# A fused attention and feed-forward kernel: RMS weight row behind the first q, last block's scores in two banks, sink scores inside score phases, one score phase merged

## The chip, the cores and the metric

The kernel runs on one core of a Trainium2 chip. The metric is the device time of that core in microseconds (us). The core has TensorE (PE in the profile, with its weight loads as PEld), VectorE (DVE), ScalarE (ACT), GpSimd (POOL) and SyncE (SP), which here only issues DMAs. POOL issues DMAs too: those that turn float32 into bfloat16 on the way.

## The reference

There are 4 sequences (b) of 768 positions, 8 heads (h) of width 64, a window of 128 and 4 sink positions.

```python
scores = scale * np.matmul(q, k.transpose(0, 1, 3, 2))
keep = (pos[None, :] < 4) | ((rel >= 0) & (rel < 128))     # rel = query - key
scores = np.where(keep, scores, -1e9)
a = softmax(scores)
attn = np.matmul(a, v)                        # 4, 8, 768, 64
x = attn as 3072 rows of 512
xn = x / sqrt(mean(x * x) + 1e-6) * rms_g
g = xn @ w_gate;  val = xn @ w_val            # 512 -> 1536
out = (g * sigmoid(g) * val) @ w_out          # 1536 -> 512, float32
```

So each query sees the four first keys of its sequence and the 128 latest keys.

## The kernel before, in words

The 3072 rows are cut into 24 blocks (`g`) of 128 positions, six to a sequence (`b, t = divmod(g, 6)`). Four blocks make a group (`G`) of 512 rows for the feed-forward part (FFN); there are six groups.

**Attention of a block.** q and k of the block are loaded and transposed, for blocks 0 to 7 on PE (`pe_t`, L412, with a copy `copy_t`, L421), from block 8 on by DMA transposes that SP issues (`dma_t`, L428). `scores` (L445) multiplies the block's keys with the queries of this block and of the next, since the window reaches back into the block before; it uses four PSUM banks, two heads to a bank. Matmuls of two heads run in pairs on the two halves of PE's rows (64 partitions each). The last block of a sequence (t = 5) has no next block, and fills half of each of its four banks. `exps` (L463) is ACT's exponential, one for each bank; `mask_dve` or, from block 16 on, `mask_pool` cuts the window. `av` (L501) multiplies with v, where a column of ones gives the sum for the softmax. From t = 2 on the sinks lie outside the window, and `av` begins with a matmul for them. Their scores come from `sink_s` (L619), a separate phase of four PE matmuls, each on 32 columns of PE; it makes the sink scores of two blocks at once in sequences 0 and 1, of four blocks (t = 2 to 5) in sequences 2 and 3, and needs those blocks' transposed q. `sink_e` is its exponential.

**Norm.** `normal` (L526), `square` (L537) and `rms` (L545) divide by the softmax's sum and form the RMS norm. The weight row `rms_g` is loaded into one partition (`grow`, L341), spread over 128 partitions by one matmul with ones (`unit_gb`, L398) and scaled by ACT to `gb` (`scale_gb`), which `rms` reads. The block's x is then transposed, on PE for blocks 0 to 8 (`pe_x`, L575), by a DMA transpose on SP from block 9 on (`dma_x`, L590).

**FFN of a group.** A unit (`ffn`, L832) is 16 times 128, 8 times 256 or 4 times 512 columns of g and as many of v, each in a bank; then tanh on ACT (L764) and two DVE operations (L770, L780) give hT. Group 0 is worked in four chunks of 128 rows, groups 1 and 2 in two of 256, the rest whole: 12 units in each group. `project` (L786) multiplies hT with wo, ACT takes the result out of PSUM and SP stores it.

**Who sets the order.** All operations are first given to a planner (`Plan`, L27): each with a cost in ns, what it needs and gives, the banks that it takes and drops, and a priority. The planner walks through time: of all operations whose needs are met it takes the one that can start earliest, with the lower priority number first where two are equal. It models DMA rings too. The resulting list is emitted, so that every engine then runs its instructions in that fixed order. There are eight PSUM banks; an operation that takes k banks can start when k are free. Fill matmuls (`warm`, 30 of them) have the last priority of all.

Needs of note:

- `gate_of(g)` (L640): a block from `GATE_FROM` on scores only after FFN unit `(g // 4 - 1) * 18 + 4 * (g % 4) - GATE_LEAD` (18 units to a group: 12 of FFN and 6 for the projection).
- A DMA transpose of block g's q or k is issued only after the scores of block `g - T_LEAD`, a load of block g (from 10 on) only after the scores of block `g - LOAD_LEAD`.
- The list `LOADS` (L177) is the order of POOL's loads; eight may be under way (`DEPTH`). `w-9-12` loads columns 9 to 12 (in units of 128) of w_gate and then of w_val.
- SP's first three DMAs are in the order of their priorities: k of block 0 (-90), `grow` (-89.5), q of block 0 (-89).

Of the kernel before, what the change touches and what calls it, by code (L numbers as in the profile page):

```python
# [26 lines left out]
class Plan:  # L27
# [3 lines left out]


    LATE = 300
    HOP = {"PE": 40, "ACT": 35, "DVE": 35, "POOL": 90, "SP": 60}
    START = {"PE": 800, "ACT": 800, "DVE": 1030, "POOL": 1290, "SP": 800}

# [32 lines left out]
    def run(self):  # L69
        free, users = dict(self.START), {}  # L70
        self.loads = sum(o["ring"] == "POOL" for o in self.ops)
        wait = {o["at"]: set(o["needs"]) for o in self.ops}
        cand = {e: [] for e in free}
        left = len(self.ops)
        for o in self.ops:
            for t in o["needs"]:
                users.setdefault(t, []).append(o)
            if not o["needs"]:
                for e in o["ways"]:
                    cand[e].append(o)  # L80
        busy, warm, mode, order = [], False, 0, []
        while left:
            first = None
            for e, found in cand.items():
                for o in found:
                    k = len(o["takes"])
                    if k > len(self.banks):
                        continue
                    ready = o["ready"] + self.HOP[e] if o["ready"] else 0
                    if k:  # L90
                        ready = max(ready, sorted(self.banks.values())[k - 1] + 40)
                    start = max(free[e], ready)
                    key = (start, o["prio"], ready, o["at"])
                    if first is None or key < first[0]:
                        first = key, e, o
            if first is None:
                raise RuntimeError("stuck: %s" % [
                    (o["gives"], list(wait[o["at"]])) for o in self.ops if o["at"] in wait
                ][:20])
            (start, *_), e, o = first  # L100
            for x in o["ways"]:
                cand[x].remove(o)
            wait.pop(o["at"])
            left -= 1
            ns, lat, fn = o["ways"][e]
            if e == "PE":
                busy = [(a, d) for a, d in busy if a > start - 3413]
                warm = start - free[e] < 4000 and (warm or sum(d for a, d in busy) > 3000)
                ns = ns if warm else 2 * ns
                if o["mode"] != mode:  # L110
                    ns, mode = ns + 110, o["mode"]
                busy.append((start, ns if mode != 2 else 0))
                lat = ns + 180
            for s in o["takes"]:
                i = min(self.banks, key=lambda i: (self.banks[i], i))
                del self.banks[i]
                self.held[s] = i
            free[e] = start + ns
            end = start + lat
            if o["ring"] is not None:  # L120
                end = self.land(o["ring"], end, o["work"]) + self.LATE
            for s in o["drops"]:
                self.banks[self.held[s]] = end + 12
            for t in o["gives"]:
                for x in users.pop(t, ()):
                    x["ready"] = max(x["ready"], end + 12)
                    w = wait[x["at"]]
                    w.discard(t)
# [8 lines left out]
def kernel(  # L137
# [195 lines left out]
    for i, name in enumerate(F32_LOADS):  # L333
# [5 lines left out]
                "ACT": (640, lambda n=n, g=g: cast(n, g, nc.scalar.copy))},  # L339
               [(n + "st", g), "table"], [(n, g)], -99)  # L340
    op({GROW: (430, 1000, lambda: {"SP": nc.sync, "ACT": nc.scalar}[GROW].dma_start(  # L341
        out=grow, in_=moe_rms_g.rearrange("(o d) -> o d", o=1)))}, (), ["grow"], -89.5,
        ring="HW", work=50)
    act(1290, None, (), ["table"], -80)

# [99 lines left out]
    def scores(g, n0, n1):  # L445
        b, t = divmod(g, NT)
        qkT = T["qkT", b]
        for u in range(2):
            for j in range(2):
                hp = 2 * u + j  # L450
                for hi in range(2):
# [8 lines left out]
                        start=g >= PE_MASKS, stop=True, skip_group_check=True,  # L460
                    )

    def exps(g, u, hi, n0, n1, last):  # L463
        if ("e", g, u) not in T:
            T["e", g, u] = epool.tile([P, 4, 2, P], BF16, name=f"e{u}", bufs=3)
# [35 lines left out]
    def av(g, u):  # L501
# [7 lines left out]
        for j in range(2):  # L509
            for hi in range(2):  # L510
# [3 lines left out]
                if t >= 1:  # L514
                    nc.tensor.matmul(  # L515
                        out=dest, lhsT=T["e", g - 1, u][:, x, 1, :],
                        rhs=V16[b][:, t - 1, h, :],
                        start=(t == 1), stop=False, skip_group_check=True,
                    )
                nc.tensor.matmul(  # L520
                    out=dest, lhsT=T["e", g, u][:, x, 0, :], rhs=V16[b][:, t, h, :],
                    start=(t == 0), stop=True, skip_group_check=True,
                )
        T.pop(("e", g - 1, u), None)
# [104 lines left out]
    def sink_e(b, t, n):  # L629
# [17 lines left out]
    for g in range(NB):  # L647
        b, t = divmod(g, NT)
# [17 lines left out]
                   [(n, g)] + old + [("s", g - T_LEAD)], [(n + "T", g)], g,  # L666
                   ring="TR", work=1000)

        slots = [("s", g, u, hi) for u in range(2) for hi in range(2)]
        parts = [(0, 1), (1, 2)] if g in SPLIT else [(0, nq)]  # L670
        if g < PE_MASKS:
            pe(864, lambda g=g: mask_bias(g), [("bias", 0), ("bias", 1), "ident", "idnos"]
               + ([("qp", g), ("kp", g)] if g else []), [("mb", g)], pa, takes=slots)
        for n0, n1 in parts:
            needs = [("kT", g)] + [("qT", g + i) for i in range(n0, n1)] + gate_of(g)
            needs += [("mb", g)] if g < PE_MASKS else []
            last = (n0, n1) == parts[-1]
            pe(220 * (n1 - n0), lambda g=g, n=(n0, n1): scores(g, *n), needs,
               [("s", g, n0)] + ([("s", g)] if last else []), pa + 1 + n0,
               takes=slots if g >= PE_MASKS and n0 == 0 else (), mode=1)  # L680
            for u in range(2):
                for hi in range(2):
                    act(215 * (n1 - n0) + 55,
                        lambda g=g, u=u, hi=hi, n=(n0, n1), last=last: exps(g, u, hi, *n, last),
                        [("s", g, n0), "table"] + ([("av", g - 2, u)] if g >= 2 else [])
                        + ([("x", g, u, 0, n0)] if hi else []),
                        [("x", g, u, hi, n) for n in range(n0, n1)], early,
                        drops=[("s", g, u, hi)] if last else ())
        for u in range(2):
            xs = [[("x", g, u, hi, n) for hi in range(2)] for n in range(nq)]  # L690
            if g < PE_MASKS:
                es = xs
# [10 lines left out]
            T["es", g, u] = es  # L703
            needs = es[0] + (T["es", g - 1, u][1] if t else []) + [("v", g), ("vone", b)]
            needs += [("v", g - 1)] if t else []
            needs += [("esk", b, t), ("vsk", b, 0), ("vsk", b, 1)] if t >= 2 else []
# [25 lines left out]
        if t == 0:  # L732
# [3 lines left out]
            for half in range(2):  # L736
# [6 lines left out]
            for t0, n in ((2, 2), (4, 2)) if b < 2 else ((2, 4),):  # L743
# [175 lines left out]
```

The softmax here doesn't subtract the row's maximum and nothing guards it: scores larger than these inputs give would overflow.

## Time and profile before

| what | value |
|---|---|
| median of 11 runs | 247.49 us (246.79 to 248.01) |
| the profiled execution's own time | 248.05 us |
| span of that execution, first to last instruction | 246.3 us |
| PE busy | 235.4 us (96%) |
| DVE busy | 183.7 us (75%) |
| ACT busy | 131.0 us (53%) |
| POOL busy | 88.6 us (36%) |
| FFN's matmuls: g, v (L757) and o (L790), busy | 69.5, 71.0 and 62.7 us |
| HBM read and written | 28.31 and 6.29 MB |

A row of the busiest groups reads: line, engine, operation, output and inputs with their shapes, count, then busy us and the mean ns of one, then the engine's idle time before them. Matmuls are pipelined, and a matmul's mean is longer than the distance to the next: an o matmul of 512 columns has a mean of 380 ns, while its successor starts 216 ns after it. What PE's work costs is therefore read from start to start. Records of some matmuls are missing (263 of 276 o matmuls are there). The mean granted clock is 1.00 over the span; the first 18 us still show matmuls at half rate, 107 ns for 128 columns in place of 56.

### The profile page before, as it was taken

The page shows a single profiled execution, that of the slowest core. Times are in us where ns is not written, and L with a number is a line of the kernel's source. Part 1 is how long each engine was busy: PE and PEld are TensorE (multiplying, and loading weights), DVE is VectorE, ACT ScalarE, POOL GpSimd, SP SyncE. Part 2 cuts the span into 40 slices and gives each one's busy share as a digit, 9 for nine tenths or more (in the row PEclk, how much of TensorE's full clock was granted, in tenths as well). Part 3 has the DMA queues.
Part 4 walks back from the last instruction along what each step waited for, and adds up shares of the span by engine and source line. Part 5 has one row for each costly group of instructions (what it writes and reads, how often), then busy time and mean ns, then how long its engine had stood idle before and what let it go on. Part 6 is the DMA issues. An engine that isn't in the chain of part 4 may idle for free.

```text
span 246.3 us, 5510 instructions
## 1 busy us (share of the span) xinstructions
PE 235.4 (96%) x2098; PEld 149.4 (61%) x2120; DVE 183.7 (75%) x482; ACT 131.0 (53%) x276; POOL 88.6 (36%) x114
## 2 busy tenths in 40 slices
PE   4798999999999999999999999999999999999994
PEld 2467998785788775588875444444545444444443
DVE  4178979997899998899889589992299993377700
ACT  3559456778677556555627445834736621333211
POOL 8986755696444559522003300221604100000000
PEclk9999999999999999999999999999999999999999
DMA  7999999999999999999923644013320013200022
GB/s 103 172 168 196 192 187 189 154 140 169 160 199 133 142 128 157 167 203 156 154 23 85 145 107 94 3 21 87 109 64 20 6 21 106 85 3 0 0 85 85
DMA packets 111979, 27.22 MB, mean 110 GB/s; under 512 B 102097, under 2 KB 109009, under 8 KB 111954
## 3 DMA queue, kind: packets, MB, share of 16 engines
q0 software_dynamic: 80704, 13.90, 77.3%
q1 hardware_dynamic: 31106, 12.85, 27.8%
q8 instruction: 16, 0.26, 0.5%
q10 hardware_dynamic: 144, 0.13, 0.2%
q14 instruction: 9, 0.07, 0.1%
HBM read 28.31 MB, written 6.29 MB: 140 GB/s over the span
## 4 chain that ended last, share of the span: by engine, by line
PE 80%; DVE 10%; DMA 4%; issue 3%; ACT 2%; SPq 0%; DVEq 0%; ACTq 0%
PE v L757 21%; PE g L757 21%; PE o L790 21%; PE s L456 4%; DVE hT L780 2%; PE av L520 2%; DMA stage<-in_q_dram 2%; DVE p L770 2%; DVE r L560 2%; DMA xnt<-xr 2%; PE av L515 2%; DVE xr L564 2%; PE av L505 1%; PE o_last L808 1%; DVE x L532 1%
## 5 line engine op out<-in xcount | busy, mean ns | idle before, releaser
L757 PE MATMUL v<-xnt,wv 128*128 128x128 bf16 (+2 forms) x522 | 71.0, 281 | 0.3
L757 PE MATMUL g<-xnt,wg 128*128 128x128 bf16 (+2 forms) x525 | 69.5, 282 | 0.5 <-DMA xnt<-xr 0.4
L764 ACT ACTIVATE th<-g 128x512 bf16<-128x512 f32 x72 | 42.9, 600 | 45.8 <-PE g L757 42.0
L790 PE MATMUL o<-wo,hT 128*128 128x512 bf16 x263 | 62.7, 380 | 1.2 <-issue 0.6
L770 DVE SCALAR_TENSOR_TENSOR p<-th,g 128x512 bf16<-128x512 bf16 x72 | 48.0, 682 | 15.2 <-ACT th L764 14.8
L757 PEld LDWEIGHTS <-wg 128*128 128x128 bf16 x528 | 43.0, 98 | 19.6 <-issue 0.6
L757 PEld LDWEIGHTS <-wv 128*128 128x128 bf16 x528 | 42.6, 98 | 18.5 <-issue 0.8
L469 ACT ACTIVATE e<-s 128x512 bf16<-128x512 f32 (+1 forms) x104 | 48.2, 541 | 8.2 <-PE s L456 8.0
L780 DVE TENSOR_TENSOR hT<-p,v 128x512 bf16<-128x512 bf16 x72 | 47.2, 681 | 1.5 <-PE v L757 0.6
L790 PEld LDWEIGHTS <-hT 128*128 128x128 bf16 x276 | 25.5, 98 | 28.7 <-issue 1.3
L491 POOL TENSOR_SCALAR_AFFINE_SELECT e<-e 128x512 bf16<-128x512 bf16 x14 | 9.4, 678 | 65.2 <-ACT e L469 52.2
L798 ACT ACTIVATE osb<-o 128x512 f32<-128x512 f32 x23 | 13.8, 598 | 29.1 <-PE o L790 29.1
L327 POOL DMA_DIRECT2D v<-in_v_dram x24 | 21.3, 888 | 14.5 <-DMA q<-in_q_dram 8.2
L323 POOL DMA_DIRECT2D q<-in_q_dram x23 | 20.5, 893 | 12.4 <-DMA k<-in_k_dram 3.9
L323 POOL DMA_DIRECT2D k<-in_k_dram x23 | 20.4, 886 | 11.3 <-DMA wo<-in_moe_w_out_dram 3.3
L532 DVE TENSOR_TENSOR x<-av,rden 128x256 bf16<-128x256 f32 x48 | 20.4, 424 | 1.6
L531 DVE RECIPROCAL rden<-av 128x4 f32<-128x4 f32 x48 | 8.5, 176 | 17.1 <-PE av L520 17.1
L540 ACT ACTIVATE sq<-x 128x512 bf16<-128x512 bf16 x24 | 15.1, 631 | 9.7 <-DVE x L532 9.6
L486 DVE TENSOR_TENSOR e<-e,masks 128x1024 bf16<-128x1024 bf16 (+1 forms) x30 | 18.9, 650 | 0.9 <-ACT e L469 0.8
L564 DVE SCALAR_TENSOR_TENSOR xr<-x,r,gb 128x512 bf16<-128x512 bf16 x24 | 19.0, 790 | 0.9
L520 PE MATMUL av<-v,e 128*128 128x65 bf16 x192 | 17.3, 197 | 0.0
L456 PE MATMUL s<-qkT 64*128 64x256 bf16 (+1 forms) x208 | 14.8, 266 | 0.6 <-ACT qkT L423 0.6
(70 smaller groups left out, 183.1 us busy)
## 6 DMA issues: line engine op xcount, KB each, us to landing
out_dram<-osb SPq DMA_DIRECT2D x23, 256.0 KB, 2.2
v<-in_v_dram POOLq DMA_DIRECT2D x24, 128.0 KB, 10.3
q<-in_q_dram POOLq DMA_DIRECT2D x23, 128.0 KB, 10.4
k<-in_k_dram POOLq DMA_DIRECT2D x23, 128.0 KB, 10.4
wo<-in_moe_w_out_dram POOLq DMA_DIRECT2D x2, 768.0 KB, 12.4
wg<-in_moe_w_gate_dram POOLq DMA_DIRECT2D x4, 256.0 KB, 7.2
wv<-in_moe_w_val_dram POOLq DMA_DIRECT2D x4, 256.0 KB, 7.9
wg<-in_moe_w_gate_dram POOLq DMA_DIRECT2D x1, 384.0 KB, 10.2
```

The lines of the kernel that those rows point to most:

```text
L323: nc.gpsimd.dma_start(out=T[name, g], in_=block_of(src, g))
L327: nc.gpsimd.dma_start(out=V16[b][:, t, :, 0:D], in_=block_of(v, g))
L456: nc.tensor.matmul(out=BANK[slot][:, j * 256 + n0 * P:j * 256 + n1 * P], lhsT=qkT[pr, 1, hp, t * P:(t + 1) * P], rhs=qkT[pr, 0, hp, (t + n ...
L469: nc.scalar.activation(out=T["e", g, u][:, 2 * hi:2 * hi + 2, n0:n1, :].rearrange("p x n c -> p x (n c)"), in_=ps.rearrange("p (j c) -> p ...
L520: nc.tensor.matmul(out=dest, lhsT=T["e", g, u][:, x, 0, :], rhs=V16[b][:, t, h, :], start=(t == 0), stop=True, skip_group_check=True,)
L532: nc.vector.tensor_tensor(out=T["x16", g][:, 4 * u:4 * u + 4, :], in0=pvv[:, :, 0:D], in1=rden.unsqueeze(2).to_broadcast((P, 4, D)), op=AL ...
L564: nc.vector.scalar_tensor_tensor(out=T["xr", g], in0=T.pop(("x16", g)).rearrange("p h d -> p (h d)"), scalar=r[:, 3:4], in1=gb, op0=ALU.mu ...
L757: nc.tensor.matmul(out=ps[:, i * n:(i + 1) * n], lhsT=w_sb[:, kt, ft * P:(ft + 1) * P], rhs=T["xnt", G][:, kt, cols], start=(kt == 0), sto ...
L764: nc.scalar.activation(out=T["th", key], in_=BANK[("g", key)], func=ACT.Tanh, scale=0.5,)
L770: nc.vector.scalar_tensor_tensor(out=T["p1", key], in0=T.pop(("th", key)), scalar=1.0, in1=BANK.pop(("g", key)), op0=ALU.add, op1=ALU.mult,)
L780: nc.vector.tensor_tensor(out=T[hk][:, i:i + n, cols], in0=T.pop(("p1", key)).rearrange("p (n c) -> p n c", n=n), in1=BANK.pop(("v", key)) ...
L790: nc.tensor.matmul(out=BANK[("o", G, tb)], lhsT=T["h", G, ft // 4][:, ft % 4, tb * P:(tb + 1) * P], rhs=wo[:, ft, :], start=(ft == 0), sto ...
```

## The change

Eight things are changed.

1. `grow` gets priority -80, so SP issues it behind q of block 0.
2. `w-9-12` becomes `w-9-10 w-10-12`: four loads in place of two.
3. `X_DMA_FROM` goes from 9 to 8: block 8's x is transposed by DMA and not on PE.
4. The last block of a sequence gets functions of its own: eight matmuls into two banks, four heads to a bank; two exponentials of 512 columns in place of four of 256; two masks over 512 columns. `av` reads the new tile.
5. From sequence 2 on (`FUSE_FROM`) the sink scores are no operation of their own: they are emitted at the end of the score phase of block t = 2, whose needs and banks grow by theirs (the transposed q of t = 2 to 5, one bank).
6. `MERGE = (2,)`: the last block of sequence 2 (block 17) has no score phase of its own; its matmuls are put ahead of those of block 18, and the needs and banks of both are joined.
7. `GATE_FROM` 6 to 8, `GATE_LEAD` 6 to 14, `LOAD_LEAD` 9 to 10, `T_LEAD` 3 to 4.
8. The planner gets `RESERVE = 8`: when an operation that takes more than 8 banks is waiting, one with a later priority may not take banks that it would need.

The loop over the blocks keeps its needs otherwise; the part that makes the scores moves into a function `block_scores`.

```diff
+    RESERVE = 8
...
+            many = min(
+                (o for o in cand["PE"] if len(o["takes"]) > self.RESERVE), default=None,
+                key=lambda o: o["prio"],
+            )
...
+                    if (k and many and o["prio"] > many["prio"] and start > many["ready"]
+                            and len(self.banks) - k < len(many["takes"])):
+                        continue
...
-    LOADS = "q-1 k-1 v-0 w-0-2 v-1 qkv-2 qkv-3 w-2-4 w-4-6 w-6-8 w-8-9 w-9-12 qkv-4 wo-0-6 qkv-5 wo-6-12 qkv-6 qkv-8 qkv-7"
+    LOADS = "q-1 k-1 v-0 w-0-2 v-1 qkv-2 qkv-3 w-2-4 w-4-6 w-6-8 w-8-9 w-9-10 w-10-12 qkv-4 wo-0-6 qkv-5 wo-6-12 qkv-6 qkv-8 qkv-7"
-    X_DMA_FROM = 9
+    X_DMA_FROM = 8
-    GATE_FROM = 6
-    LOAD_LEAD = 9
+    GATE_FROM = 8
+    LOAD_LEAD = 10
-    GATE_LEAD = 6
-    T_LEAD = 3
+    GATE_LEAD = 14
+    T_LEAD = 4
+    FUSE_FROM = 2
+    GROW_PRIO = -80
+    MERGE = (2,)
...
-        out=grow, in_=moe_rms_g.rearrange("(o d) -> o d", o=1)))}, (), ["grow"], -89.5,
+        out=grow, in_=moe_rms_g.rearrange("(o d) -> o d", o=1)))}, (), ["grow"], GROW_PRIO,
...
+    def scores_last(g):
...
+        for hp in range(HP):
+            for hi in range(2):
+                pr = slice(hi * D, (hi + 1) * D)
+                nc.tensor.matmul(
+                    out=BANK["s", g, hi][:, hp * P:(hp + 1) * P], lhsT=qkT[pr, 1, hp, cols],
+                    rhs=qkT[pr, 0, hp, cols], start=True, stop=True, skip_group_check=True,
+                )
+    def exps_last(g, hi):
...
+        nc.scalar.activation(
+            out=T["el", g][:, hi * HP:(hi + 1) * HP, :].rearrange("p x c -> p (x c)"),
+            in_=BANK.pop(("s", g, hi)), func=ACT.Exp, scale=inv_sqrt_d,
+        )
...
+    def sink_parts(b):
+        return ((2, 2), (4, 2)) if b < 2 else ((2, 4),)
+    def sink_needs(b, t, n):
+        return [("ksk", b)] + [("qT", b * NT + t + i) for i in range(n)]
...
+            if merged and n0 == 0:
+                more, banks, given, other = merged
+                needs, gives, takes = needs + more, gives + given, takes + banks
+                work.insert(0, lambda g=other: scores_last(g))
...
+            if last and b >= FUSE_FROM:
+                for t0, n in sink_parts(b):
+                    if t0 == t:
+                        needs = needs + sink_needs(b, t0, n)
+                        gives.append(("ss", b, t0))
+                        takes = takes + [("ss", b, t0)]
+                        work.append(lambda b=b, t0=t0, n=n: sink_s(b, t0, n))
...
+            if b in MERGE:
+                merged = (needs, slots, [("s", g, 0), ("s", g)], g)
+            else:
+                pe(220, lambda g=g: scores_last(g), needs, [("s", g, 0), ("s", g)], pa + 1,
+                   takes=slots, mode=1)
...
-                pe(n * 53 + 16, lambda b=b, t0=t0, n=n: sink_s(b, t0, n),
-                   [("ksk", b), ("s", g + 1)] + [("qT", g + t0 + i) for i in range(n)],
-                   [("ss", b, t0)], -1000.0 + 10 * (g + t0) + 2, takes=[("ss", b, t0)], mode=3)
+                if b < FUSE_FROM:
+                    pe(n * 53 + 16, lambda b=b, t0=t0, n=n: sink_s(b, t0, n),
+                       [("s", g + 1)] + sink_needs(b, t0, n), [("ss", b, t0)],
+                       -1000.0 + 10 * (g + t0) + 2, takes=[("ss", b, t0)], mode=3)
```

More of the change, by code (lines that the diff above doesn't have):

```diff
@@ L461, in scores, with mask_dve_last, mask_pool_last @@
                     )
+    def scores_last(g):
+        b, t = divmod(g, NT)
+        qkT = T["qkT", b]
+        cols = slice(t * P, (t + 1) * P)
+        for hi in range(2):
+            bank(("s", g, hi))
+        for hp in range(HP):
+            for hi in range(2):
+                pr = slice(hi * D, (hi + 1) * D)
[4 more added lines that the diff above has]
+    def exps_last(g, hi):
+        if ("el", g) not in T:
+            T["el", g] = epool.tile([P, H, P], BF16, name="e0", bufs=3)
+        nc.scalar.activation(
+            out=T["el", g][:, hi * HP:(hi + 1) * HP, :].rearrange("p x c -> p (x c)"),
+            in_=BANK.pop(("s", g, hi)), func=ACT.Exp, scale=inv_sqrt_d,
+        )
+    def mask_dve_last(g, hi):
+        ev = T["el", g][:, hi * HP:(hi + 1) * HP, :]
+        nc.vector.tensor_tensor(
+            out=ev, in0=ev, in1=masks[:, 1, 0:1, :].to_broadcast((P, HP, P)), op=ALU.mult,
+        )
+    def mask_pool_last(g, hi):
+        ev = T["el", g][:, hi * HP:(hi + 1) * HP, :]
+        nc.gpsimd.affine_select(
+            out=ev, in_=ev, compare_op=ALU.is_ge,
+            fill=0.0, base=0, pattern=[[0, HP], [1, P]], channel_multiplier=-1,
+        )
     def exps(g, u, hi, n0, n1, last):
@@ L519, in av @@
                     )
+                own = (T["e", g, u][:, x, 0, :] if t + 1 < NT
+                       else T["el", g][:, hi * HP + 2 * u + j, :])
                 nc.tensor.matmul(
-                    out=dest, lhsT=T["e", g, u][:, x, 0, :], rhs=V16[b][:, t, h, :],
+                    out=dest, lhsT=own, rhs=V16[b][:, t, h, :],
                     start=(t == 0), stop=True, skip_group_check=True,
@@ L645, in gate_of, with block_scores @@
         return [("F", G, i)] if i < FTN else [("O", G, (i - FTN) * 2 // 3)]
-    for g in range(NB):
+    merged = None
+    def block_scores(g):
+        nonlocal merged
         b, t = divmod(g, NT)
@@ L651 @@
         early = -20.0 + g if g < 2 * GB else 0.1 * g
-        old = []
-        if b >= 2:
-            old = [("s", NT * (b - 2) + i) for i in range(NT)]
-            old += [("ss", b - 2, i) for i in ((2, 4) if b - 2 < 2 else (2,))]
-        for n in "qk":
-            if g < QK_DMA_FROM:
-                pe(225, lambda n=n, g=g: pe_t(n, g), [(n, g), "ident"] + old, [(n + "p", g)],
-                   pa, takes=[(n, g)])
-                ways = {"DVE": (345, lambda n=n, g=g: copy_t(n, g, nc.vector.tensor_copy)),
-                        "ACT": (470, lambda n=n, g=g: copy_t(n, g, nc.scalar.copy))}
-                either(ways, [(n + "p", g), "table"], [(n + "T", g)], early, drops=[(n, g)])
-            else:
-                sp(1290, 1200, lambda n=n, g=g: dma_t(n, g),
-                   [(n, g)] + old + [("s", g - T_LEAD)], [(n + "T", g)], g,
-                   ring="TR", work=1000)
         slots = [("s", g, u, hi) for u in range(2) for hi in range(2)]
@@ L677 @@
             last = (n0, n1) == parts[-1]
-            pe(220 * (n1 - n0), lambda g=g, n=(n0, n1): scores(g, *n), needs,
-               [("s", g, n0)] + ([("s", g)] if last else []), pa + 1 + n0,
-               takes=slots if g >= PE_MASKS and n0 == 0 else (), mode=1)
+            gives = [("s", g, n0)] + ([("s", g)] if last else [])
+            takes = slots if g >= PE_MASKS and n0 == 0 else []
+            ns, work = 220 * (n1 - n0), [lambda g=g, n=(n0, n1): scores(g, *n)]
+            if merged and n0 == 0:
+                more, banks, given, other = merged
+                needs, gives, takes = needs + more, gives + given, takes + banks
+                work.insert(0, lambda g=other: scores_last(g))
+                ns += 220
+                merged = None
+            if last and b >= FUSE_FROM:
[5 more added lines that the diff above has]
+                        work.append(lambda b=b, t0=t0, n=n: sink_s(b, t0, n))
+                        ns += 53 * n + 100
+            pe(ns, lambda work=work: [w() for w in work], needs, gives, pa + 1 + n0, takes=takes,
+               mode=1)
             for u in range(2):
@@ L703 @@
             T["es", g, u] = es
+    for g in range(NB):
+        b, t = divmod(g, NT)
+        nq = 2 if t + 1 < NT else 1
+        pa = -1000.0 + 10 * g
+        early = -20.0 + g if g < 2 * GB else 0.1 * g
+        old = []
+        if b >= 2:
+            old = [("s", NT * (b - 2) + i) for i in range(NT)]
+            old += [("ss", b - 2, i) for i in ((2, 4) if b - 2 < 2 else (2,))]
+        for n in "qk":
+            if g < QK_DMA_FROM:
+                pe(225, lambda n=n, g=g: pe_t(n, g), [(n, g), "ident"] + old, [(n + "p", g)],
+                   pa, takes=[(n, g)])
+                ways = {"DVE": (345, lambda n=n, g=g: copy_t(n, g, nc.vector.tensor_copy)),
+                        "ACT": (470, lambda n=n, g=g: copy_t(n, g, nc.scalar.copy))}
+                either(ways, [(n + "p", g), "table"], [(n + "T", g)], early, drops=[(n, g)])
+            else:
+                sp(1290, 1200, lambda n=n, g=g: dma_t(n, g),
+                   [(n, g)] + old + [("s", g - T_LEAD)], [(n + "T", g)], g,
+                   ring="TR", work=1000)
+        if t + 1 == NT:
+            slots = [("s", g, hi) for hi in range(2)]
+            needs = [("kT", g), ("qT", g)] + gate_of(g)
+            if b in MERGE:
+                merged = (needs, slots, [("s", g, 0), ("s", g)], g)
+            else:
+                pe(220, lambda g=g: scores_last(g), needs, [("s", g, 0), ("s", g)], pa + 1,
+                   takes=slots, mode=1)
+            xs = []
+            for hi in range(2):
+                act(480, lambda g=g, hi=hi: exps_last(g, hi),
+                    [("s", g, 0), "table"] + [("av", g - 2, u) for u in range(2)]
+                    + ([("x", g, 0)] if hi else []), [("x", g, hi)], early, drops=[("s", g, hi)])
+                if g < POOL_MASK_FROM:
+                    dve(335, lambda g=g, hi=hi: mask_dve_last(g, hi), [("x", g, hi), "masks"],
+                        [("e", g, hi)], early)
+                else:
+                    pool(590, lambda g=g, hi=hi: mask_pool_last(g, hi), [("x", g, hi)],
+                         [("e", g, hi)], g)
+                xs.append(("e", g, hi))
+            T["es", g, 0] = T["es", g, 1] = [xs]
+        else:
+            block_scores(g)
+        for u in range(2):
+            es = T["es", g, u]
             needs = es[0] + (T["es", g - 1, u][1] if t else []) + [("v", g), ("vone", b)]
@@ L742 @@
                     [("vsk", b, half)], 0.1 * g, drops=[("vs", b, half)])
-            for t0, n in ((2, 2), (4, 2)) if b < 2 else ((2, 4),):
-                pe(n * 53 + 16, lambda b=b, t0=t0, n=n: sink_s(b, t0, n),
-                   [("ksk", b), ("s", g + 1)] + [("qT", g + t0 + i) for i in range(n)],
-                   [("ss", b, t0)], -1000.0 + 10 * (g + t0) + 2, takes=[("ss", b, t0)], mode=3)
+            for t0, n in sink_parts(b):
+                if b < FUSE_FROM:
+                    pe(n * 53 + 16, lambda b=b, t0=t0, n=n: sink_s(b, t0, n),
+                       [("s", g + 1)] + sink_needs(b, t0, n), [("ss", b, t0)],
+                       -1000.0 + 10 * (g + t0) + 2, takes=[("ss", b, t0)], mode=3)
                 act(n * 107 + 55, lambda b=b, t0=t0, n=n: sink_e(b, t0, n),
```

## The prediction

> **What bounds the kernel now.** I began with the page's first two parts: who is busy, and when.
>
> ```profile
> span 246.3 us, 5510 instructions
> PE 235.4 (96%) x2098; PEld 149.4 (61%) x2120; DVE 183.7 (75%) x482; ACT 131.0 (53%) x276; POOL 88.6 (36%) x114
> ...
> PE   4798999999999999999999999999999999999994
> ...
> DVE  4178979997899998899889589992299993377700
> ```
>
> PE is full in all but the first four slices (25 us) and the last. So I asked next what PE waits for once it is running, in the waits of PE alone from 22.5 us on:
>
> ```profile
> PE o L790 <- issue: 0.6, 4, 0.2
> PE x L579 <- DVE xr L564: 0.4, 1, 0.4
> PE g L757 <- DMA xnt<-xr: 0.4, 1, 0.4
> ```
>
> That is all: 1.4 us in 220. Three of the four "issue" waits are first records missing from a project group (a group of 11 or 7 in place of 12 or 8). Measured from start to start, two real stalls remain: at 141.00 (the last attention matmul starts at 140.44 and could have been followed 0.03 later: 0.53 us) and at 205.35 (two o matmuls 0.51 apart, not 0.216: 0.29 us). Together 0.82 us. The kernel therefore ends when PE has started plus the sum of PE's work. A change can gain in three ways only: start sooner, give PE less work, remove those stalls. It loses by any new wait on PE.
>
> The start I read in the chain of waits of the first 26 us:
>
> ```profile
> 0.81 0.46 SPq L315
> 1.27 0.06 issue
> 1.33 0.46 SPq L341
> 1.79 0.06 issue
> 1.84 5.17 DMA stage<-in_q_dram
> 7.01 0.02 issue
> 7.03 0.63 ACT q L319
> ```
>
> SP issues k, then the weight row (L341), then q, and the chain goes through all three, then through q's landing at 7.01.
>
> **The change part by part.** The sum is made against the profiled execution, 248.05 us (span 246.3 and 1.75 around it); the median of the runs is 247.49, so that execution lies 0.56 above it, and I subtract the same amount from the median.
>
> *Weight row behind q.* q is issued 0.52 us sooner (0.46 + 0.06). Does it land sooner? The windows of that stretch (last columns: DMA share, GB/s) say so:
>
> ```profile
> 2.40:3.00 0.60, 0.00 (x0) 0.00 (x0) 0.20 (x1) 0.00 (x0) 0.59 (x2) 1.00 1.13 259
> 3.40:3.90 0.50, 0.00 (x0) 0.00 (x0) 0.17 (x2) 0.00 (x0) 0.49 (x3) 1.00 0.31 66
> ```
>
> k moves at 259 GB/s, and then the DMA engines are nearly empty before q is in full flow: q came late, it did not queue. The skill's "DMA: Bandwidth & Descriptors" (Queues, rings and completion order) speaks against this part: one issuing engine's transfers are taken in ring order on each DMA engine, so q stays behind k whenever it is issued. By that rule alone the gain is 0; by the row up to 0.5. I follow the row, but what comes next caps it: PE's order goes on from block 0's q to block 1's q and k, and that k (issued at 2.65, landing 5.5 later) is there at 8.16, while its transposes start at 8.53 now. So 0.37 is passed on at most, somewhat more if the software loads land sooner too. Then the clock: four x transposes take 0.57 us at 17.45 and 0.40 at 22.77, so PE is at half rate until nearly 18 us. "TensorE: Matmul & The Clock Gate" (Part 1) says that the window which releases the clock runs free and does not begin with the work. By the rule, work drawn ahead of 18 us is still done at half rate, so the shift is worth half (0.18); by the chain alone 0.37. I take 0.25, ends 0 and 0.5. The row itself, now last on SP's queue, should land near 7.2; its matmul runs at 9.74 and the scaled row is first read at 15.80: cost 0, and without that cover at most PE's wait for it, 0.1.
>
> *Weights 9 to 12 in two loads.* Two more POOL issues of 0.74. POOL waits there for DMAs anyway (1.05, 0.85 and 0.43 us at 20.9 to 24.9), so 0. The loads behind land later: one ft alone took 0.72 us from landing to landing, three together 1.92, so I estimate 1.36 for two and 0.16 more for each of wg and wv, 0.3 in all. Cover: the second half of wo lands at 44.91, and its matmul starts at 45.99; 1.1 us, less the 0.25 above. Cost 0; bare, 0.3.
>
> *Block 8's x by DMA.* PE loses four transposes at 0.056: **0.22** gained. A copy (427 ns on DVE or 600 on ACT) goes too. A DMA transpose joins SP's queue among q, k transposes and stores (about 1.2 us of issue). These x transposes land within 2.4 to 7.9 us; block 8's row is ready at 80.7 and first used after 103. Cost 0.
>
> *Last block's scores in two banks.* The same eight matmuls. ACT has two exponentials of 606 in place of four of 393: 0.36 less, four times, 1.4 us of ACT at 53% busy, off the path: 0. The mask work is the same. Two banks come free sooner: nothing I can count.
>
> *Fused sinks and the merged phase.* What a switch of tile shape costs is read between starts:
>
> ```profile
> 108.85 1.04 PE L757 MATMUL g<-xnt,wg 128*128 128x256 bf16 x8
> 109.82 0.61 PE L456 MATMUL s<-qkT 64*128 64x256 bf16 x8
> 110.36 0.20 PE L515 MATMUL av<-v,e 128*128 128x65 bf16 x1
> ...
> 173.71 0.40 PE L622 MATMUL ss<-qkT,ksk 128*32 128x512 bf16 x4
> 174.04 0.61 PE L456 MATMUL s<-qkT 64*128 64x256 bf16 x8
> 174.59 1.04 PE L790 MATMUL o<-wo,hT 128*128 128x512 bf16 x4
> ```
>
> Eight g at 0.109 are 0.87, but the scores start 0.97 later: 0.10 to go in. Four pairs at 0.107 are 0.43, but the next starts 0.54 later: 0.11 to come out. From sink to score 0.33, of which 0.22 is streaming: 0.11 as well. So a sink beside scores needs three switches, apart four: fusing saves one, **0.10**, for sequence 2 (its sink stands alone at 127.07). Sequence 3's already touches a score phase at 173.71: 0. Merging block 17's scores into block 18's saves one entry and one exit: **0.20**.
>
> What they add is waits. Block 14's score phase now needs q transposed up to block 17, block 20's up to 23, and PE works in order: FFN matmuls, av and all ACT's exponentials behind it stand with it. That is why the lead of the transposes must grow from 3 to 4, since block 17's transposes would otherwise wait for block 14's own scores. Block 17's scores wait for block 18's transposes and for six of the eight banks at once (one FFN unit holds two for about 2 us: tanh 600, two DVE operations of 682).
>
> *Gates and leads.* No work is added or removed; attention may run eight FFN units (14 us at 1.73 each) ahead of now. The nearest row is the present order: 0.82 us of stall. The stall at 141.00 is block 15's x transpose landing just in time, after blocks 14 to 16 had all waited for the sink scores at 127.07; an earlier sink takes that away. Ends: 0.8 gained, or about 2 lost in a new wait. I take half of the stalls gained, **0.4**. The new reserve of banks acts only on operations with over 8 banks, and the largest here takes six: nothing.
>
> Sum: 0.25 + 0.22 + 0.10 + 0.20 + 0.40 = 1.17, so 248.05 becomes 246.9 (span 245.1) and the median 247.49 becomes **246.3**. 0.2% is 0.5 us, about what runs of this kernel can tell from no change.
>
> **The rivals.**
>
> *Block 14 stands on PE for block 17's transposes (slower).* Block 17's two transposes go out after block 13's scores: two issues of about 1.25, then 7.7 us to land (the median in 100 to 130 us, where loads crowd the DMAs). That is 10.2 us; blocks 13 and 14 now score at 101.95 and 109.82, 7.9 apart. If the new order keeps that spacing, PE stands 2.3 us, and the stall gain goes too: 246.3 + 0.4 + 2.3 = 249.0. It decides from a spacing below 10.2 us. For it: nothing in the trace has PE depend on a transpose so soon. Against: the same planner set the present order, and no row has PE waiting for qkT past 21 us. Block 20's landings are short by then (2.4 us). Chance 0.13.
>
> *DVE becomes the bound.* From 60 to 130 us:
>
> ```profile
> 60.00:130.00 70.00, 69.53 (x693) 53.06 (x695) 63.90 (x167) 41.77 (x88) 28.66 (x33) 1.00 1.73 146
> ```
>
> DVE, the third pair, has 6.1 us free in 70. 14 us ahead is about two blocks more in this stretch, each with 2 x (0.176 + 0.424) + 1.85 = 3.05 us of DVE work: exactly full. If it overflows by half a block, PE waits 1.5: 246.3 + 0.4 + 1.5 = 248.2. Against: those blocks' masks are POOL's, and FFN's DVE work goes ahead of theirs. Chance 0.07.
>
> *Nothing but the counted work.* q lands when it did and the stalls come back elsewhere: 247.49 - 0.52 = 247.0; with the 0.3 of the weight loads uncovered, 247.3. Chance 0.20.
>
> *The start gives more.* From 18 to 23 us PE stands 1.0 us and runs ten fill matmuls (0.56). If the order closes two thirds of that (1.0) as well: 245.3. Chance 0.15.
>
> **How the numbers follow.** The case of the sum has 0.45, from 245.8 to 246.95. Faster: 0.45 + 0.15 = 0.60; within 0.2%: 0.20; slower: 0.13 + 0.07 = 0.20. Signs agree in most of it, yet the tail of the first rival is long: the range 245.2 to 248.6 leaves out about half of the best case and most of the worst, under 0.2.
>
> **What would show it.** q's cast starts near 6.5 instead of 7.03 and block 0's first scores near 8.85 instead of 9.20. PE busy falls by about 0.5 us. The lone sink phase at 127 is gone and there is one score phase less. PE's waits have no row for xnt; block 15's x is ready well before its FFN. I am wrong if PE shows a wait for qkT ahead of a score phase of block 14, if hT or g rows of PE wait for DVE between 60 and 130 us, or if q still lands at 7.0.

## The result and the profile after

The changed kernel takes 245.44 us (median of 12 runs, 245.03 to 246.37), the kernel before on the same chips 247.09 (47 runs, 246.23 to 248.24): a ratio of 0.9931, 95% interval 0.992 to 0.9943, or 1.7 us. Forecast were 1.2 us and the same direction. The profiled executions are 248.05 and 245.11 us, one near the top of its kernel's runs and the other near the bottom, so the two profiles lie 2.9 us apart: their difference must not be read as the gain.

The first lines of the page of the changed kernel:

```profile
span 243.4 us, 5493 instructions
PE 232.7 (96%) x2096; PEld 148.3 (61%) x2116; DVE 181.0 (74%) x481; ACT 130.9 (54%) x268; POOL 89.4 (37%) x116
...
PE   4968999999999999999999999999999999999994
...
PEclk9979999999999999999999999999999999999999
```

PE is as full as before, and the third slice (12.2 to 18.3 us) shows a granted clock of 0.7: the rate at which PE was allowed to run, as a share of the full one. The last section comes back to it. From 22.5 us on, all that is left of PE's waits is one line, where three stood before:

```profile
PE o L896 <- issue: 0.2, 1, 0.2
```

The waits for xr and for xnt are gone. SP's first three issues, and the two windows that the prediction read, both of the changed kernel:

```profile
0.81 0.45 SPq L327 DMA_DIRECT2D stage<-in_k_dram  x1
1.32 0.56 SPq L327 DMA_DIRECT2D stage<-in_q_dram  x1
1.93 0.67 SPq L353 DMA_DIRECT2D grow<-in_moe_rms_g_dram  x1
```

```profile
2.40:3.00 0.60, 0.00 (x0) 0.00 (x0) 0.20 (x1) 0.00 (x0) 0.58 (x2) 1.00 1.08 247
3.40:3.90 0.50, 0.00 (x0) 0.00 (x0) 0.17 (x2) 0.00 (x0) 0.49 (x3) 1.00 1.09 244
```

q is issued 0.52 us sooner, and the hole of 3.4 to 3.9 us (66 GB/s before) is filled at the rate of k (244 GB/s). q lands at 6.06 in place of 7.01. But PE's order of the start is another one. Before:

```profile
7.70 1.03 PE L416 MATMUL q<-ident,q 128*128 128x128 bf16 x8 [1.25 <-ACT q L319]
...
9.20 0.61 PE L456 MATMUL s<-qkT 64*128 64x128 bf16 x8
9.74 2.07 PE L399 MATMUL gb<-grow,ones 1*128 1x512 f32 x2
11.74 0.61 PE L456 MATMUL s<-qkT 64*128 64x128 bf16 x8
```

After:

```profile
6.75 0.87 PE L428 MATMUL q<-ident,q 128*128 128x128 bf16 x8 [0.30 <-ACT q L331]
7.55 1.12 PE L411 MATMUL gb<-grow,ones 1*128 1x512 f32 x2
8.61 0.62 PE L468 MATMUL s<-qkT 64*128 64x128 bf16 x16
...
13.78 0.19 PE L569 MATMUL av<-v,e 128*128 128x65 bf16 x1 [1.50 <-DMA v<-in_v_dram]
...
21.14 0.40 PE L628 MATMUL x<-ident,xr 128*128 128x128 bf16 x4 [0.57 <-DVE xr L613]
```

The weight row's matmul now stands ahead of block 0's scores; before, it stood between their two parts, at 9.74. Further on PE waits 1.5 us for block 1's v.

To keep start and rest apart I read two times from each trace: the first v matmul of FFN, and from there to the last matmul of all. Up to the first v, all the traces in the table have done the same work on PE.

| trace | first v, us | from there to the last matmul, us |
|---|---|---|
| before | 23.06 | 219.56 |
| changed | 21.38 | 218.41 |
| row's priority alone | 21.79 | 219.37 |
| old order, q early | 21.05 | 219.21 |
| new order, q late | 22.76 | 219.41 |
| new leads alone | 22.62 | 219.28 |
| changed, old start | 20.07 | 218.89 |
| changed, no fuse, no merge | 19.91 | 219.63 |
| changed, no merge, four banks | 21.60 | 219.85 |
| changed, old gates | 20.18 | 227.48 |
| changed, loads in one | 21.46 | 218.48 |

The first column is one execution's and moves with the clock (the kernel before scatters by 2 us over its runs). The second runs at the full clock in all but one trace and is steadier; still, kernels that share one order after the start scatter by 0.35 there with the order of before, and by 0.5 with the changed one. A very early start also gives some of itself back. With the first v at 19.91, PE's weight loads then wait for wg's DMA, which a later start doesn't meet:

```profile
24.11 1.34 PEld L863 LDWEIGHTS <-wg 128*128 128x128 bf16 x24 [0.39 <-DMA wg<-in_moe_w_gate_dram]
30.02 1.06 PEld L863 LDWEIGHTS <-wg 128*128 128x128 bf16 x19 [0.32 <-DMA wg<-in_moe_w_gate_dram]
```

These waits are 0.7 of the 1.2 us by which that trace's second column exceeds the changed kernel's.

### The profile page after: what moved, and what is told of

Same layout as the page of the kernel before. It is cut to its first block, busy times and chain, and to the rows that moved or that the text cites. A ratio compares the mean times of both kernels' runs of the same rounds, so it can differ in the third digit from the quotient of the medians.

```text
span 243.4 us, 5493 instructions
## 1 busy us (share of the span) xinstructions
PE 232.7 (96%) x2096; PEld 148.3 (61%) x2116; DVE 181.0 (74%) x481; ACT 130.9 (54%) x268; POOL 89.4 (37%) x116
## 4 chain that ended last, share of the span: by engine, by line
PE 78%; DMA 15%; POOL 2%; issue 1%; ACT 1%; DVE 0%; POOLq 0%
PE o L896 23%; PE v L863 22%; PE g L863 22%; DMA wv<-in_moe_w_val_dram 7%; DMA q<-in_q_dram 5%; PE s L468 3%; DMA v<-in_v_dram 3%; PE av L569 2%; PE av L562 1%; PE av L552 1%; PE o_last L914 1%; POOL wg L381 1%; POOL wv L381 1%; ACT e L516 1%; PE ss L671 0%
## 5 line engine op out<-in xcount | busy, mean ns | idle before, releaser
L896 PE MATMUL o<-wo,hT 128*128 128x512 bf16 x263 | 63.9, 379 | 0.8 <-issue 0.2
L516 ACT ACTIVATE e<-s 128x512 bf16<-128x512 f32 (+1 forms) x88 | 43.9, 572 | 6.0 <-PE s L468 4.7
L335 POOL DMA_DIRECT2D q<-in_q_dram x23 | 20.5, 892 | 14.6 <-DMA k<-in_k_dram 5.9
L613 DVE SCALAR_TENSOR_TENSOR xr<-x,r,gb 128x512 bf16<-128x512 bf16 x24 | 18.0, 751 | 0.9
L569 PE MATMUL av<-v,e 128*128 128x65 bf16 x192 | 17.0, 194 | 1.6 <-DMA v<-in_v_dram 1.5
L533 DVE TENSOR_TENSOR e<-e,masks 128x1024 bf16<-128x1024 bf16 x26 | 17.1, 685 | 1.2 <-ACT e L516 1.2
L538 POOL TENSOR_SCALAR_AFFINE_SELECT e<-e 128x512 bf16<-128x512 bf16 x10 | 6.3, 634 | 31.0 <-ACT e L516 15.5
L562 PE MATMUL av<-v,e 128*128 128x65 bf16 x160 | 15.0, 194 | 0.0
L569 PEld LDWEIGHTS <-e 128*128 128x128 bf16 x192 | 13.2, 98 | 2.7 <-issue 0.2
```

The source lines that it names most:

```text
L335: nc.gpsimd.dma_start(out=T[name, g], in_=block_of(src, g))
L516: nc.scalar.activation(out=T["e", g, u][:, 2 * hi:2 * hi + 2, n0:n1, :].rearrange("p x n c -> p x (n c)"), in_=ps.rearrange("p (j c) -> p ...
L562: nc.tensor.matmul(out=dest, lhsT=T["e", g - 1, u][:, x, 1, :], rhs=V16[b][:, t - 1, h, :], start=(t == 1), stop=False, skip_group_check=True,
L569: nc.tensor.matmul(out=dest, lhsT=own, rhs=V16[b][:, t, h, :], start=(t == 0), stop=True, skip_group_check=True,)
L613: nc.vector.scalar_tensor_tensor(out=T["xr", g], in0=T.pop(("x16", g)).rearrange("p h d -> p (h d)"), scalar=r[:, 3:4], in1=gb, op0=ALU.mu ...
L896: nc.tensor.matmul(out=BANK[("o", G, tb)], lhsT=T["h", G, ft // 4][:, ft % 4, tb * P:(tb + 1) * P], rhs=wo[:, ft, :], start=(ft == 0), sto ...
```

## The experiments

Twelve kernels ran, each with five rounds against the kernel before on its chip.

**The start: is it q's landing, or the order?** The row's priority alone:

```diff
-        ..., ["grow"], -89.5,
+        ..., ["grow"], -80,
```

> The kernel before with the weight row's priority alone changed (-80). The prediction's theory, earlier landing of q and no more: 0.25 us faster, 0.5 at most, ratio near 0.999. Rival, the planner's new order of the start (the weight row's matmul ahead of block 0's scores, both score parts in one stretch, block 1's k transposes behind them): 0.5 to 1.7 us faster, ratio 0.993 to 0.998, with the first FFN matmul clearly before 21.3 us. Second rival, the dense part carries all of the gain: ratio 1.000.

246.45 against 246.83 us, ratio 0.9987 (0.9975 to 0.9999): 0.3 us faster. The planner's list is new on PE, DVE and ACT through the start, and the same after it. So landing and order were taken apart, by exchanging two entries of the finished list:

```diff
     order = plan.run()
+    i, j = [next(n for n, x in enumerate(order) if w in x[4]["gives"]) for w in ("grow", ("qst", 0))]
+    a, b_ = list(order[i]), list(order[j])
+    a[3], b_[3] = b_[3], a[3]
+    order[i], order[j] = tuple(a), tuple(b_)
```

Only what the two entries issue (`[3]`) changes places.

> The kernel before with every engine's order kept, and SP's second and third DMA exchanged by hand, so that q is issued ahead of the weight row. If q's landing makes the gain: q lands near 6.1 and the time falls by as much as in the run with the row's priority changed. If the order makes it: q lands near 6.1 too, but the time falls by 0 to 0.3 us only, since PE still has block 1's k and the weight row's matmul ahead of block 0's second score part.

245.88 against 246.83, ratio 0.9961 (0.9946 to 0.9976): almost 1.0 us faster, with the order on PE, DVE, ACT and POOL unchanged. PE's start of this kernel:

```profile
6.25 1.06 PE L416 MATMUL q<-ident,q 128*128 128x128 bf16 x8
7.13 0.52 PE L416 MATMUL k<-ident,k 128*128 128x128 bf16 x4
7.64 0.40 PE L456 MATMUL s<-qkT 64*128 64x128 bf16 x8
7.96 1.12 PE L399 MATMUL gb<-grow,ones 1*128 1x512 f32 x2
9.02 0.47 PE L456 MATMUL s<-qkT 64*128 64x128 bf16 x8
...
14.27 0.61 PE L416 MATMUL q<-ident,q 128*128 128x128 bf16 x4 [2.32 <-DMA q<-in_q_dram]
```

Block 0's first scores start at 7.64 (8.61 in the changed kernel, where the row's matmul is ahead of them). The 2.32 us at 14.27 show the next bound: block 2's q, a load that POOL issues, isn't there yet.

> The run with the row's priority changed, every engine's order kept, but the two DMAs exchanged back, so that q is issued last, as in the kernel before. If the order makes the gain: most of the gain of that run stays (0.3 us or more faster than before). If q's landing makes it: no faster than before, ratio 1.000.

This is the planner's new order of the run with the row's priority alone, with q issued last again. 247.86 against 246.83, ratio 1.0038 (1.0022 to 1.0053): 0.9 us slower. So the order alone costs 0.9 us, the early q alone gains 1.0, and both together gain 0.3. The rival that gave the gain to the order is dead: the order is a loss that the early q pays for.

**The leads without the fused phases.**

```diff
-    GATE_FROM = 6
-    LOAD_LEAD = 9
-    GATE_LEAD = 6
-    T_LEAD = 3
+    GATE_FROM = 8
+    LOAD_LEAD = 10
+    GATE_LEAD = 14
+    T_LEAD = 4
```

> The kernel before with the gates and leads of the change alone (gate from 8, gate lead 14, load lead 10, transpose lead 4). By the prediction's sum the stall at 141.0 (0.53 us) or the one at 205.4 (0.29) goes, 0.4 of both taken: ratio near 0.998; the separate sink of sequence 2 still waits for block 17's q, so the stall at 141 may stay and the ratio be 0.999. By the rival in which DVE fills up between 60 and 130 us: slower, 1.002 to 1.006, with PE waiting for hT.

247.13 against 246.83, ratio 1.0013 (1.0003 to 1.0024): not faster, if anything slower. The stalls at 141 and 205 are gone from its trace, but a new one stands at 89, between the sink's v matmul (vs) and FFN's:

```profile
89.09 0.39 PE L604 MATMUL vs<-v,sel 128*128 128x260 bf16 x2
89.79 1.03 PE L757 MATMUL v<-xnt,wv 128*128 128x256 bf16 x8 [0.31 <-DVE p L770]
```

From start to start it is 0.48 us. p is the first of the two DVE operations behind tanh, the last that reads a bank of g; so PE waits for a bank here.

**The old start inside the changed kernel.** The planner sees the row at -89.5 again, and the two issues are exchanged as above:

> The changed kernel with the start's order of the kernel before on every engine (row at -89.5 for the planner), and SP's second and third DMA exchanged by hand, so that q is still issued ahead of the row. Theory now: start and dense part add. Early q in the old order gave -0.95 us, the dense part of the change about -1.15: ratio to before 0.9915, some 245.0 us, 0.5 below the changed kernel. Rival, the new start order fits the changed dense part better: no faster than the changed kernel (0.993).

244.79 against 247.03, ratio 0.9913 (0.9883 to 0.9943; six runs). As the sum said (0.9915), though the interval holds the changed kernel's 0.9931 too.

**Loads.** On top of that, and then in the changed kernel alone:

```diff
-    LOADS = "q-1 k-1 v-0 w-0-2 v-1 qkv-2 qkv-3 ...
+    LOADS = "q-1 k-1 v-0 v-1 q-2 k-2 w-0-2 v-2 qkv-3 ...
```

> The run before this one, and block 1's v and block 2's q and k are loaded ahead of the first weights. If the software loads are what holds the start once q is early (PE stood 2.3 us for block 2's q at 14.3): PE's wait there goes, first FFN matmul 0.3 to 1 us sooner, ratio to before 0.988 to 0.990. If the first weights become late instead: the first FFN matmul stands for w and nothing is gained or 0.5 us lost.

> The changed kernel with block 1's v and block 2's q and k loaded ahead of the first weights, and nothing else. In the changed kernel PE stood 1.5 us for block 1's v at 13.8. If that is on the path: ratio to before 0.990 to 0.992. If the norm's chain of block 0 and 1 sets the first FFN matmul anyway: the same as the changed kernel, 0.993.

Ratios 0.9934 (0.9914 to 0.9954) and 0.9946 (0.9927 to 0.9964): nothing gained either time. PE's wait for v is gone; in its place PE waits 1.0 us for block 0's row (xr), and then for block 3's q and k (1.1 and 0.7 us in the first of the two, 0.7 and 0.3 in the second). In both traces the granted clock then falls to half, from 17.1 and 17.6 us until 20.5 and 21.0, through most of FFN's first g matmuls.

**Without the fused and the merged phase** (`FUSE_FROM = 4`, `MERGE = ()`):

> The changed kernel with the sink scores in phases of their own again and block 17's scores in a phase of their own (two banks kept, new leads kept). By the prediction: 0.30 us of switches come back and the stall of 0.53 us near 141 may with them: 0.3 to 0.8 us slower than the changed kernel, ratio to before 0.994 to 0.9965. Rival, the leads alone do it: only the 0.3, 0.9945.

246.05 against 247.03, ratio 0.9952 (0.9931 to 0.9973), 0.5 us less gain than the changed kernel's, within the two intervals. Its trace has no wait for a bank after the first v, and 49 changes of tile shape on PE after the first v, as the kernel before; the changed kernel has 45.

**The row's matmul behind block 0's scores:**

```diff
-    pe(1000, unit_gb, ["ones", "grow"], ["gbm"], GB_PRIO, takes=[("gb",)], mode=2)
+    pe(1000, unit_gb, ["ones", "grow", ("s", 0)], ["gbm"], GB_PRIO, takes=[("gb",)], mode=2)
```

> The changed kernel with one more need: the weight row's matmul waits for block 0's second score part, so the planner can't put it ahead of block 0's scores. If its place ahead of the scores is what costs the changed kernel part of the early q: as fast as the changed kernel with the start's old order (ratio 0.990 to 0.992), block 0's row ready about 2 us sooner than at 15.8. If its place doesn't matter: as the changed kernel, 0.993.

244.75 against 246.72, ratio 0.9924 (0.991 to 0.9938; six runs). Block 0's row (xr) is written from 14.15 on, in place of 15.8. This and the old start have the lowest medians of all, 2.0 and 2.2 us below the kernel before, but neither interval is clear of the changed kernel's.

**The changed kernel with the old gates** (`GATE_FROM = 6`, `GATE_LEAD = 6`, `LOAD_LEAD = 9`; `T_LEAD` stays 4):

> The changed kernel with the gates and load lead of the kernel before (gate from 6, gate lead 6, load lead 9); the transpose lead stays 4, which the fused sink needs. By the prediction the earlier attention removed stalls: they come back, 0.3 to 0.5 us slower than the changed kernel, 0.9945 to 0.995. Rival: with the sink scored early there is nothing left to stall, and the gates are worth nothing (0.993); the new leads alone in the kernel before gained nothing (1.0013).

252.67 against 246.72, ratio 1.0246 (1.0225 to 1.0266): 7.2 us lost against the changed kernel by the medians, 7.8 by the ratios. Its windows around 141 us (the last three columns: granted clock, DMA share, GB/s):

```profile
137.00:141.50 4.50, 1.16 (x6) 0.31 (x4) 3.36 (x16) 1.32 (x3) 0.00 (x0) 0.96 0.40 99
141.50:148.00 6.50, 5.95 (x15) 2.12 (x16) 3.09 (x7) 1.19 (x2) 0.00 (x0) 0.50 0.44 103
```

and the matmuls there:

```profile
136.27 1.89 PE L896 MATMUL o<-wo,hT 128*128 128x512 bf16 x8
142.05 3.57 PE L863 MATMUL g<-xnt,wg 128*128 128x512 bf16 x8 [3.90 <-DMA xnt<-xr]
145.42 3.17 PE L863 MATMUL v<-xnt,wv 128*128 128x512 bf16 x8
148.42 1.89 PE L863 MATMUL g<-xnt,wg 128*128 128x512 bf16 x8
```

Block 14's scores with the sinks in them come at 127.4 (112.5 in the changed kernel; in the kernel before, 109.8 for the scores and 127.1 for the sinks). Block 15's row is written at 138.7 (126.1), and group 3's FFN stands until its transpose has landed. The granted clock is half for nearly 7 us from 141.2 on: eight g take 3.4 us from start to start, later ones 1.7. Start to start the wait is 4.06, and the 16 matmuls behind it take 6.4 us in place of 3.5: 7.0 of the 9.1 us by which this trace's second column exceeds the changed kernel's. Another 1.7 are shorter waits: v for ACT's exponential 0.7, q 0.6, wg 0.4. Gates and load lead were not tried apart.

**No merge, and the last block in four banks again** (`MERGE = ()`, and the last block goes through the same function as the others):

> The changed kernel with the last block's scores in four banks and block 17's phase of its own; the sinks stay fused. By the prediction: 0.20 us for the two switches of block 17, and nothing for the banks: ratio 0.994. Rival, the freed banks and the shorter exponentials let FFN's matmuls run on: 0.4 us or more slower, 0.9945 and above, with PE stalls beside last blocks' scores.

247.02 against 246.72, ratio 1.0011 (0.9998 to 1.0025): the whole gain is gone, 2.0 us (intervals added: 1.4 to 2.6). PE after the score phase of block 12:

```profile
87.90 0.61 PE L468 MATMUL s<-qkT 64*128 64x256 bf16 x8
89.03 0.39 PE L653 MATMUL vs<-v,sel 128*128 128x260 bf16 x2 [0.53 <-DVE p L876]
89.63 1.03 PE L863 MATMUL v<-xnt,wv 128*128 128x256 bf16 x8 [0.21 <-DVE p L876]
```

Both wait for p again: PE is short of banks, at the start of the next sequence. From start to start the two waits are 0.59 and 0.38, together 1.0 us of the 1.44 by which the second column exceeds the changed kernel's. The two switches of the merge are 0.2 more (47 changes of shape in place of 45), and a wait for block 2's row at 28 us about 0.3. No trace with the new leads and the last block in two banks has a wait for p after the first v.

**Weights 9 to 12 in one load each:**

> The changed kernel with the weights 9 to 12 in one load each again. By the prediction 0, since the loads' 0.3 us was covered by 1.1 us; now that the start is earlier and PE waits for loads at 25 and 46 us, it may be up to 0.3 us faster: ratio 0.992 to 0.993. If the split was made for a reason that I don't see (the first of the columns comes sooner): slower, 0.994 or more.

245.28 against 246.72, ratio 0.994 (0.9918 to 0.9963): the same as the changed kernel as far as this can tell.

## Why the prediction was right, and where it was not

*What bounds the kernel*: held. Start of PE, PE's work, PE's stalls: every gain and loss above is one of the three, if the clock at which the work runs is counted with it.

*Weight row behind q (0.25 taken, 0 to 0.5)*: the landing was mis-sized. Early q in an unchanged order is worth 1.0 us (0.6 to 1.3), twice my upper end. The ring-order rule, from which I read a gain of 0, held for the order (k landed at 4.10, q behind it at 6.06) and not for the gain: q filled the hole behind k. I capped the gain by block 1's k, landing at 8.16; but with q out of the way that load lands sooner as well (7.39 in the changed kernel, 7.06 with the old order), and the full clock came by about 9.5 us in 8 of 11 traces with the early q, and not before 15 in the three with the late one. I had halved the gain, since a window that runs free would leave the end of the half rate where it was; in these traces it moved by far more than q did. They don't decide whether the window runs free. Nor does the record show what lets the clock rise sooner: the shorter gap on PE ahead of q's transposes is a guess, which was not tried by itself. With the row's priority alone that gap was gone as well, and the full clock came at 15.1.

The other half of this step failed outright: "PE's order goes on from block 0's q to block 1's q and k", and the row's matmul costs 0. The planner, which models the row as landing later, put its matmul ahead of block 0's scores. The new order as a whole costs 0.6 (row's priority alone against the old order with early q) to 0.9 us (new order, q late). The row's place is the likely cause, but the run that changed its need alone is not clear of the changed kernel. The two errors had opposite signs: 0.25 stood where about 0.3 was measured, and that they agree is luck.

*Block 8's x by DMA (0.22)*: 24 x transposes are on PE after the first v in place of 28, and there is no wait for xnt: as costed, though not tried alone. *Loads (0)*: right within what the run could tell.

*Fused sinks and merged phase (0.30)*: four changes of shape fewer, one more than I had counted, at 0.1 each: 0.4. The merged phase in the changed kernel:

```profile
130.99 1.03 PE L896 MATMUL o<-wo,hT 128*128 128x512 bf16 x4
131.95 0.40 PE L484 MATMUL s<-qkT 64*128 64x128 bf16 x8
132.19 0.60 PE L468 MATMUL s<-qkT 64*128 64x256 bf16 x8
```

Block 17's eight matmuls go over into block 18's after 0.24 us, with nothing between.

*Last block in two banks (0)*: as a gain over the kernel before, 0 may stand, since that kernel has no wait for p after the first v. What the prediction missed is that the new leads need the two banks. Both kernels with the new leads and four banks wait for a bank at 89 us, 0.48 us (new leads alone) and 1.0 us (no merge, four banks); the changed kernel doesn't, nor does the one with two banks, no fuse and no merge, which lost only 0.5. I had called it "nothing I can count" because ACT wasn't the bound; what counts is how many banks are left to FFN while ACT works. No run changed the banks alone, and each edit moves the whole list, so how much of the 2.0 is theirs stays open beyond the 1.0 that the trace shows.

*Gates and leads (0.40)*: the stalls did go, 0.82 us of them before and about 0.2 after. But "attention may run ahead" gains nothing by itself (1.0013 alone, with the wait for a bank in its place). It is the price of the fused sinks: without it block 14's scores come 15 us later, and 7 to 8 us are lost. The first rival named the right danger in the wrong place. The planner let block 15's scores go ahead of block 14's, so that 16.9 us lie between blocks 13 and 14 (95.7 and 112.5), and PE never waited for one of SP's transposes of q. With the old gates it didn't either; attention as a whole was late, and the bill came at the next group's x.

*The sum*: start 0.3 and rest 1.15 (trace to trace, 219.56 to 218.41) make 1.5 of the 1.7 measured; the remainder is within the intervals. In the trace the rest is the counted work: 0.22 for the x transposes, 0.4 for changes of shape and 0.6 for stalls are 1.2. Put on the forecast's base, the ratio gives 245.8 us, at the edge of my main case (245.8 to 246.95). The rival nearest in number, "the start gives more" (245.3), isn't what happened: the start's net was 0.3 (row's priority alone), and 1.15 came after the start. "DVE becomes the bound" didn't come either, as no row of PE waits for DVE after 22.5 us. PE's busy time fell by 2.7 us and not by 0.5, but 2.5 of that lies ahead of the first v, where more of the work ran at the full clock.

## What to carry to other kernels

In a kernel with a planned order a priority is two changes: what the hardware does sooner, and what the planner makes of it. Take them apart by keeping the list and exchanging two entries by hand; here one gained 1.0 us and the other lost 0.9. A change that makes one phase wait for more (the fused sinks) needs the lead that feeds it to grow with it, and that lead can look useless when it is tried alone. Count scarce buffers as a resource of the engine that fills them: with the new leads, four banks for a last block in place of two stood beside waits of 1.0 us, more than the 0.6 us of work on PE that the change saved.

## What the runs showed of the hardware

An idle PE of 4.06 us at 138 us (changed kernel with the old gates) was followed by matmuls at half rate, with a granted clock of 0.50 for about 6.8 us, so the wait cost 7.0 us in all. In the changed kernel's own start the 1.5 us wait for v is followed by the same: 128-column matmuls are 56 ns apart from 7.3 us on, 107 from about 14.2 to 17.5, and 56 again. But a wait of that length needn't do it. In the changed kernel with the old start PE waits as long, and the granted clock stays full:

```profile
13.54 0.40 PE L428 MATMUL q<-ident,q 128*128 128x128 bf16 x4 [1.55 <-DMA q<-in_q_dram]
```

A DMA issued 0.52 us sooner (block 0's q) landed 0.95 us sooner. It moved at 244 GB/s from 3.4 to 3.9 us, and POOL's loads moved their first packets at 4.1 us; the late q moved at 66 GB/s in that window and shared the DMA engines with POOL's loads from 3.7 us on.
